# One fp32 attention and two feed-forward stages on one core: the last four blocks of the first feed-forward become two Strassen pairs

## The chip, the cores and the metric

The kernel runs on one core of one Trainium2 chip. The metric is the device time of one execution in microseconds (us), taken as the median over runs. Times of single instructions below come from one profiled execution of the kernel before the change.

## What is computed

```python
def _attn_ref(q, k, v, g_norm):            # 8 batches, 8 heads, 576 tokens, 64 wide
    kv = np.einsum('bhsd,bhse->bhde', k, v)
    out = np.einsum('bhsd,bhde->bhse', q, kv)
    rms = np.sqrt(np.mean(out * out, axis=-1, keepdims=True) + 1e-06)
    return out / rms * g_norm
def _moe_ref(x, w1, w2, w3, w_out):        # x 4608 x 512, w1..w3 512 x 768, w_out 768 x 512
    h = np.maximum(np.maximum(x @ w1, x @ w2), x @ w3)
    return h @ w_out
def _moe2_ref(x, w_in, w_out, s, b):       # w_in 512 x 2048, w_out 2048 x 512
    r = np.maximum(x @ w_in, 0.0)
    return (s * (r * r) + b) @ w_out
```

The attention output, 8 x 576 = 4608 tokens of 512 numbers, is the input x of the first feed-forward, and its output that of the second. Everything is wanted in fp32.

## The kernel before

**Arithmetic.** A float is split into a rounded part and a rest (hi and lo; hi on ScalarE at L279, lo on an adder engine at L282), and a product of two matrices is three products, hi by hi, hi by lo and lo by hi (`mm3`, L161 to L163). Each matmul instruction is a 128 x 128 weight tile against 512 columns.

**Blocks.** The tokens stand in nine blocks of 512. Block bb from 0 to 7 is the first 512 tokens of batch bb; block 8 collects the 64 tokens that each batch has left over (`o_rem`). The attention of batch bb+1 is done during the first feed-forward of block bb:

- k and v are loaded and multiplied (`kvor`, L334); q is loaded by four gathers on SyncE's queue (`load_q`, L349) and transposed on VectorE (`qt`, L390);
- `ops` (L403) and `rps` are the attention's products in PSUM, copied out as `o` by ScalarE and VectorE;
- the norm of each of four 128-row parts needs a square, its hi and lo (`sqh` on VectorE, L429, `sql` on GpSimd), a matmul with a matrix of ones (`ms`, L438 and L439, one PSUM bank), three ScalarE steps (L484 to L489) and three VectorE steps (`u`, `u`, `o`, L494 to L499);
- x is split into `xh` and `xl` (L503, L509; three of four `xl` on GpSimd).

**First feed-forward.** For every block there are 18 column tiles (6 of each of w1, w2, w3) by four k-chunks by three matmuls, 216 in all, into a ring of four PSUM banks (`g1_part`, L516). `g1_out` (L524) keeps the running maximum of the three weights' products (ScalarE copies the first, VectorE takes the maximum of the others, L531); h is split, and four output tiles by six chunks by three matmuls, 72 in all, form the product with w_out (`g2_mm`, L540). Its result goes to DRAM (`x1d`).

**Second feed-forward.** It works on pairs of blocks in a Strassen-Winograd scheme: 7 products of quarter matrices in the place of 8, with sums made on VectorE and ScalarE (`product`, L933, matmuls at L947; `z_product` with L1101). Its weights are converted from raw 64-bit input during the first feed-forward (`plan_conv` jobs p0 to p31, `tr_p` in the rows) and stored in DRAM.

**What sets the order.** Each piece of work is a `job` with a position, an engine, a cost, what it reads and writes, and which ring of tiles it takes. `arrange` (L71) simulates the engines with those costs and lists the jobs in the order in which they would begin; it runs once for all jobs with a position below `CUT` (L699) and once for the rest. The order within each engine is fixed by it in the program, so an engine that waits holds up all that stands behind it. A block is `SL` = 22 positions long. SyncE issues nearly all DMAs.

Of the kernel before, what the change touches and what calls it, by code (L numbers as in the profile page):

```python
# [30 lines left out]
def attention_max_ffn_relu2_ffn(ctx: ExitStack, tc, q, k, v, g_norm, w1, w2, w3, wo, wi, w2o, s, b, out):  # L31
# [568 lines left out]
    def plan_o(bb, u, pp, turn, mm):  # L600
        for p in pp if bb >= ROWS else ():
# [3 lines left out]
            a=[("ops", f"ops{bb}.{u}"), ("g", f"rps{bb}.{u}")] if pp[0] == 2 * u else [])  # L605
# [9 lines left out]
    def plan_compact(bb, p, t, u, x, eng, o, sq):  # L615
# [713 lines left out]
```

## Time and profile before

| | us |
| --- | --- |
| median of 3 runs (1386.41 to 1390.83) | 1388.78 |
| the profiled execution | 1386.89 |
| span of the profiled execution | 1385.1 |
| TensorE busy, of that span | 1367.6 |
| VectorE busy | 894.0 |
| ScalarE busy | 741.7 |
| GpSimd busy | 127.1 |

The share of busy time is one of the whole span; stages differ, so the windows and single rows count for more than the table. The first feed-forward of block 8 starts at 612 us, and the second feed-forward's first product at about 678 us.

### The profile page before, as it was taken

The page shows a single profiled execution, that of the slowest core. Times are in us where ns is not written, and L with a number is a line of the kernel's source. Part 1 is how long each engine was busy: PE and PEld are TensorE (multiplying, and loading weights), DVE is VectorE, ACT ScalarE, POOL GpSimd, SP SyncE. Part 2 cuts the span into 40 slices and gives each one's busy share as a digit, 9 for nine tenths or more (in the row PEclk, how much of TensorE's full clock was granted, in tenths as well). Part 3 has the DMA queues.
Part 4 walks back from the last instruction along what each step waited for, and adds up shares of the span by engine and source line. Part 5 has one row for each costly group of instructions (what it writes and reads, how often), then busy time and mean ns, then how long its engine had stood idle before and what let it go on. Part 6 is the DMA issues. An engine that isn't in the chain of part 4 may idle for free.

```text
span 1385.1 us, 19411 instructions
## 1 busy us (share of the span) xinstructions
PE 1367.6 (99%) x7056; PEld 1122.9 (81%) x7056; DVE 894.0 (65%) x1489; ACT 741.7 (54%) x1320; POOL 127.1 (9%) x99
## 2 busy tenths in 40 slices
PE   7999999999999999999999999999999999999998
PEld 5777888888888888888888889888888888888888
DVE  5984626364545453426676767657888888888875
ACT  6873535243434352334557457657675656556565
POOL 0001313121222132212000000000000000000000
PEclk9999999999999999999999999999999999999999
DMA  9986291626555331030444745534585465454531
GB/s 269 285 179 134 73 188 56 174 74 160 87 143 90 92 89 38 1 122 0 165 170 158 254 151 196 200 147 164 212 304 166 143 203 152 148 176 128 187 118 50
DMA packets 221328, 202.51 MB, mean 146 GB/s; under 512 B 117168, under 2 KB 175536, under 8 KB 219056
## 3 DMA queue, kind: packets, MB, share of 16 engines
q1 hardware_dynamic: 221072, 201.02, 49.1%
q8 instruction: 55, 0.90, 0.3%
q14 instruction: 41, 0.34, 0.1%
q10 hardware_dynamic: 160, 0.26, 0.1%
HBM read 126.79 MB, written 74.45 MB: 145 GB/s over the span
## 4 chain that ended last, share of the span: by engine, by line
PE 96%; DVE 2%; ACT 1%; DMA 1%; issue 0%; SPq 0%; ACTq 0%; DVEq 0%
PE ps_a L947 14%; PE g L161 14%; PE zs_a L1101 14%; PE g L163 14%; PE g L162 14%; PE ps_b L947 7%; PE zs_b L1101 7%; PE ps_c L947 4%; PE zs_c L1101 4%; PE kvor L334 1%; PE ops L403 1%; PE ms L438 0%; PE ms L439 0%; PE qps L370 0%; DVE tr_w L255 0%; DMA out_dram<-o 0%
## 5 line engine op out<-in xcount | busy, mean ns | idle before, releaser
L161 PE MATMUL g<-xh,w_w 128*128 128x512 f32 x648 | 255.2, 394 | 0.0
L163 PE MATMUL g<-xh,w_w 128*128 128x512 f32 x648 | 252.8, 390 | 0.7 <-DVE w_w L282 0.7
L162 PE MATMUL g<-xl,w_w 128*128 128x512 f32 x648 | 252.6, 390 | 0.0
L279 ACT ACTIVATE zx<-z 128x512 fp32r<-128x512 f32 (+1 forms) x280 | 158.3, 586 | 123.9 <-PE zs_a L1101 37.6
L1101 PE MATMUL zs_a<-zx,w_q 128*128 128x512 f32 (+1 forms) x960 | 212.0, 369 | 0.4 <-DVE zx L282 0.4
L947 PE MATMUL ps_a<-x_q,w_q 128*128 128x512 f32 (+1 forms) x960 | 207.9, 370 | 0.0
L282 DVE TENSOR_TENSOR zx<-z,zx 128x512 fp32r<-128x512 f32 (+1 forms) x280 | 171.3, 633 | 55.5 <-ACT zx L279 50.9
L1101 PEld LDWEIGHTS zs_a<-zx,w_q 128*128 128x128 f32 x960 | 168.1, 188 | 31.9 <-DVE zx L282 0.6
L947 PEld LDWEIGHTS ps_a<-x_q,w_q 128*128 128x128 f32 x960 | 167.6, 188 | 31.8
L531 DVE TENSOR_TENSOR h<-g,h 128x512 f32<-128x512 f32 x108 | 74.6, 691 | 153.9 <-PE g L163 150.1
L161 PEld LDWEIGHTS g<-xh,w_w 128*128 128x128 f32 x648 | 121.6, 188 | 27.5 <-issue 0.8
L163 PEld LDWEIGHTS g<-xh,w_w 128*128 128x128 f32 x648 | 121.6, 188 | 26.8 <-DVE w_w L282 1.2
L162 PEld LDWEIGHTS g<-xl,w_w 128*128 128x128 f32 x648 | 121.7, 188 | 25.3 <-DVE xl L282 0.2
L1101 PE MATMUL zs_b<-zx,w_q 128*128 128x512 f32 (+1 forms) x480 | 109.4, 370 | 2.0 <-DVE zx L282 2.0
L279 ACT ACTIVATE h<-h 128x512 fp32r<-128x512 f32 x54 | 34.0, 630 | 135.8 <-DVE h L531 135.1
L947 PE MATMUL ps_b<-x_q,w_q 128*128 128x512 f32 (+1 forms) x480 | 105.8, 369 | 0.0
L1101 PEld LDWEIGHTS zs_b<-zx,w_q 128*128 128x128 f32 x480 | 84.5, 188 | 18.2 <-DVE zx L282 2.4
L947 PEld LDWEIGHTS ps_b<-x_q,w_q 128*128 128x128 f32 x480 | 84.0, 188 | 15.8
L282 POOL TENSOR_TENSOR h<-h,h 128x512 fp32r<-128x512 f32 x40 | 54.8, 1370 | 456.4 <-ACT h L279 456.4
L161 PE MATMUL g<-h,w_o 128*128 128x512 f32 x216 | 84.6, 392 | 0.0
L162 PE MATMUL g<-h,w_o 128*128 128x512 f32 x216 | 84.1, 389 | 0.0
L163 PE MATMUL g<-h,w_o 128*128 128x512 f32 x216 | 84.1, 389 | 0.0
(175 smaller groups left out, 1855.6 us busy)
## 6 DMA issues: line engine op xcount, KB each, us to landing
z<-gd SPq DMA_DIRECT2D x64, 512.0 KB
gd<-cs SPq DMA_DIRECT2D x96, 256.0 KB
z<-gd SPq DMA_DIRECT2D x48, 256.0 KB
x1d<-x SPq DMA_DIRECT2D x36, 256.0 KB
raw_w<-in_moe_w_dram SPq DMA_DIRECT2D x18, 511.0 KB
k<-in_k_dram SPq DMA_DIRECT2D x32, 256.0 KB
v<-in_v_dram SPq DMA_DIRECT2D x32, 256.0 KB
wd<-tr_p SPq DMA_DIRECT2D x32, 256.0 KB
```

Of the source, the lines that this page charges most:

```text
L161: nc.tensor.matmul(ps, lhsT=w[:, 0, sl], rhs=xh, start=first, stop=False)
L162: nc.tensor.matmul(ps, lhsT=w[:, 0, sl], rhs=xl, start=False, stop=False)
L163: nc.tensor.matmul(ps, lhsT=w[:, 1, sl], rhs=xh, start=False, stop=last)
L279: act(out=out, in_=src, func=AF.Copy)
L282: eng.tensor_tensor(out=out, in0=src, in1=hi.bitcast(F32), op=ALU.subtract)
L334: nc.tensor.matmul(ps[h * D:(h + 1) * D, p, :], lhsT=kc, rhs=vc, start=(c == 0), stop=(c == C))
L403: nc.tensor.matmul(st["ops", u][p % 2 * D:(p % 2 + 1) * D, h], lhsT=kv[sl, p], rhs=st["qt", p][sl, :N], start=True, stop=True)
L531: nc.vector.tensor_tensor(out=st["h", m], in0=ps, in1=st["h", m], op=ALU.max)
L947: nc.tensor.matmul(ps, lhsT=w[:, a, c], rhs=x[:, b_], start=new and k == 0 and e == 0, stop=k == HK - 1 and e == 2, skip_group_check=True)
L1101: nc.tensor.matmul(ps, lhsT=w[:, a, c], rhs=x[:, b_], start=new and k_ == 0 and e == 0, stop=k_ == 3 and e == 2, skip_group_check=True)
```

## The change

**Two kinds of block.** Blocks 0 to 4 (`ND` = 5) run the first feed-forward as before. Blocks 5 and 6, and 7 and 8, become two pairs (`FP`), each in the Strassen-Winograd scheme that the second feed-forward has: for each pair 9 groups (two weight tiles each) by 7 products by 6 matmuls, 378 in the place of 2 x 216.

**Sums.** `f_whole` and `f_sum` form the sums of weight tiles on VectorE and `f_hi`, `f_lo` split them in pair 0; they are stored to DRAM (`sd`) and read back in pair 1 in the reverse order of groups. `x_sum` and the splits of x's quarters are those of the second feed-forward. `f_comb` (ScalarE copies, VectorE adds that read PSUM) and `f_max` combine the seven products and keep the maximum. Two rings of four PSUM banks, "g" and "gl", take the products of one group each in turn. The finished h goes to DRAM (`hd`).

**w_out later.** The four output tiles of blocks 5 to 8 are done after both pairs, from h read back (`fh_load`, `fh_hi`, `fh_lo`); since the tiles of w_out are used by the pairs' sums, they go to DRAM (`wo_out`) and come back (`wo_back`).

**Attention earlier.** All attention of batches 2 to 7 and the norm of block 8 stand at `TA` = 20, every `WA` = 10 positions, stretched by `FA` = 0.8: inside blocks 1 to 4, 2.2 attentions to a block. x of blocks 2 to 8 is stored to DRAM (`x_out`, `xd`), and read back for blocks 2 to 4 (`x_back`) and for the pairs (`fx_load`). All `xl` is now VectorE's; `sqh` may be VectorE's or ScalarE's. `rps` of batches from 2 on takes the one bank of `ms`. Of the 32 conversions 22 stand in blocks 1 to 4 and 10 in the pairs.

```diff
-            st["rps", u] = psg.tile([P, N], F32, tag="g", name=f"rps_{bb}_{u}")
+            st["rps", u] = (psa if bb > 1 else psg).tile([P, N], F32, tag="ms" if bb > 1 else "g", name=f"rps_{bb}_{u}")
...
-        job(t + u, "DVE", 0.42, sq_hi, bb, p, r=[sq], w=["h" + sq], a=[("sqh", "h" + sq)])
+        job(t + u, "DVE/ACT", (0.42, 0.6), sq_hi, bb, p, r=[sq], w=["h" + sq], a=[("sqh", "h" + sq)])
...
+        plan_x_out(bb, p, t + 7.2 * u, o)
...
-    CUT = SL * B - 0.2
+    ND, TU = 5, 32
+    TA, WA, FA = 20, 10, 0.8
+    CUT = SL * (ND - 1) + 12
...
+    def f_whole(G, e):
+        w = f_tiles(G)[e]
+        r = st["R", G, e] = ring("c", f"fr_{G}_{e}")
+        tt(nc.vector, r, w[:, 0].bitcast(F32), add, w[:, 1].bitcast(F32))
...
+    def f_product(a, n, G, i):
+        q, new = -1 - a, i in (0, 1, 5)
+        if new:
+            st["fp", a, G, BANK[i]] = bank(parity(n + (i == 5)), f"fp_{a}_{G}_{BANK[i]}")
+        ps = st["fp", a, G, BANK[i]]
...
+        for k in range(HK):
+            x = st["x", q, i, k]
+            c = slice(o + k * P, o + (k + 1) * P)
+            for e, (u, v_) in enumerate(((0, 0), (0, 1), (1, 0))):
+                nc.tensor.matmul(ps, lhsT=w[:, u, c], rhs=x[:, v_], start=new and k == 0 and e == 0,
+                                 stop=k == HK - 1 and e == 2, skip_group_check=True)
...
+    def f_comb(a, G, i, e, tag):
+        c, j = G // 3, {3: 2, 4: 1, 5: 0}.get(i)
+        ps = st["fp", a, G, BANK[i]]
+        if i < 3:
+            st["fc", a, G, i] = ring(tag, f"fc_{a}_{G}_{i}")
+            act(out=st["fc", a, G, i], in_=ps, func=AF.Copy)
+            return
...
+        if i < 6:
+            tt(nc.vector, st["fh", a, c, i] if e == 0 else st["fc", a, G, j], ps, add, st["fc", a, G, j])
...
+    def f_max(a, G, i):
+        h = st["fh", a, G // 3, i]
+        tt(nc.vector, h, h, ALU.max, st["fc", a, G, 5 - i])
```

**VectorE in block 2.** The rows are VectorE's in program order. In the names the first number is the block or batch and the second the part; `qt`, `sqh`, `u` and `o` are attention, `h` the maximum of the first feed-forward, `tr_p` a conversion. Before:

```order
L531 TENSOR_TENSOR h_2_1_1922<-g1_2_4_1907,h_2_1_1922 128x512
L264 SCALAR_TENSOR_TENSOR tr_p7_1904<-tr_p7_1904 128x512
L531 TENSOR_TENSOR h_2_1_1922<-g1_2_5_1936,h_2_1_1922 128x512
L429 TENSOR_SCALAR sqh_3_1_1986<-sq_3_1_1934 128x512
L494 SCALAR_TENSOR_TENSOR u_3_0_1995<-ms_3_0_1968,u_3_0_1995 128x512
L531 TENSOR_TENSOR h_2_2_1971<-g1_2_7_1973,h_2_2_1971 128x512
L496 SCALAR_TENSOR_TENSOR u_3_0_1995<-u_3_0_1995,y_3_0_1988 128x512
L499 SCALAR_TENSOR_TENSOR o_3_0_1897<-o_3_0_1897,g_sb_66,u_3_0_1995 128x512
L531 TENSOR_TENSOR h_2_2_1971<-g1_2_8_1998,h_2_2_1971 128x512
```

After:

```order
L437 COPY o_rem_152<-rps_4_0_1976 128x64
L404 STREAM_TRANSPOSE qt_4_2_2014<-qraw_4_1658 128x576
L404 STREAM_TRANSPOSE qt_4_3_2020<-qraw_4_1658 128x576
L447 TENSOR_SCALAR sqh_4_0_2046<-sq_4_0_2016 128x512
L512 SCALAR_TENSOR_TENSOR u_3_3_2053<-ms_3_3_2028,u_3_3_2053 128x512
L514 SCALAR_TENSOR_TENSOR u_3_3_2053<-u_3_3_2053,y_3_3_2048 128x512
L517 SCALAR_TENSOR_TENSOR o_3_1_1772<-o_3_1_1772,g_sb_66,u_3_3_2053 128x512
L260 TENSOR_SCALAR tr_p6_2074<-raw_p6_2011 128x512
L576 TENSOR_TENSOR h_2_0_2071<-g1_2_1_2058,h_2_0_2071 128x512
L264 SCALAR_TENSOR_TENSOR tr_p6_2074<-raw_p6_2011,tr_p6_2074 128x512
L277 TENSOR_TENSOR tr_p6_2074<-tr_p6_2074 128x512
L576 TENSOR_TENSOR h_2_0_2071<-g1_2_2_2082,h_2_0_2071 128x512
```

Before, the maxima of block 2 stand among one batch's norm; after, those of block 2 stand among the end of batch 3's norm, the transposes and norm of batch 4, and conversions.

**TensorE where block 5 begins.** `xh`, `xl` are block 5's input, `w_w` the weights, `kvor` the k by v product of the next batch. Before:

```order
L334 MATMUL kvor_129<-v_6_3_3068,k_6_3_3066 64x64 x8
L334 MATMUL kvor_129<-vrem_127,krem_125 64x64 x2
L161 MATMUL g1_5_0_3601<-xh_5_3454,w_w_0_172 128x512
L162 MATMUL g1_5_0_3601<-xl_5_3455,w_w_0_172 128x512
L163 MATMUL g1_5_0_3601<-xh_5_3454,w_w_0_172 128x512
```

After, `x_q_-1` is the input of pair 0 and `fs` a split sum of weights, and `fp` are the products of one group in banks a, b and c:

```order
L161 MATMUL g2_4_3_3968<-h_4_5_3966,w_o_5_1164 128x512
L162 MATMUL g2_4_3_3968<-h_4_5_3966,w_o_5_1164 128x512
L163 MATMUL g2_4_3_3968<-h_4_5_3966,w_o_5_1164 128x512
L1392 MATMUL fp_0_0_a_4066<-x_q_-1_0_0_3855,w_w_0_200 128x512 x3
L1392 MATMUL fp_0_0_a_4066<-x_q_-1_0_1_3857,w_w_0_200 128x512 x3
L1392 MATMUL fp_0_0_b_4082<-x_q_-1_1_0_3895,fs_0_0_4024 128x512 x3
L1392 MATMUL fp_0_0_b_4082<-x_q_-1_1_1_3922,fs_0_0_4024 128x512 x3
L1392 MATMUL fp_0_0_c_4096<-x_q_-1_5_0_3997,w_w_0_200 128x512 x3
L1392 MATMUL fp_0_0_c_4096<-x_q_-1_5_1_4018,w_w_0_200 128x512 x3
```

The block's 216 direct matmuls are replaced by products of six matmuls each, and no attention stands among them; the product with w_out of block 4 ends right before.

**VectorE in the same stretch.** Before, in the first feed-forward of block 5:

```order
L531 TENSOR_TENSOR h_5_1_3714<-g1_5_4_3701,h_5_1_3714 128x512
L266 TENSOR_TENSOR tr_p22_3722<-tr_p22_3722 128x512
L531 TENSOR_TENSOR h_5_1_3714<-g1_5_5_3732,h_5_1_3714 128x512
L429 TENSOR_SCALAR sqh_6_1_3783<-sq_6_1_3730 128x512
L494 SCALAR_TENSOR_TENSOR u_6_0_3795<-ms_6_0_3765,u_6_0_3795 128x512
L531 TENSOR_TENSOR h_5_2_3768<-g1_5_7_3770,h_5_2_3768 128x512
L496 SCALAR_TENSOR_TENSOR u_6_0_3795<-u_6_0_3795,y_6_0_3785 128x512
L499 SCALAR_TENSOR_TENSOR o_6_0_3693<-o_6_0_3693,g_sb_66,u_6_0_3795 128x512
L531 TENSOR_TENSOR h_5_2_3768<-g1_5_8_3798,h_5_2_3768 128x512
```

After, in the third to fifth group of pair 0 (`fr` and `sf` are sums of weights, 128 x 512 and 128 x 256, `fc` and `fh` combine the products):

```order
L855 TENSOR_TENSOR fr_4_1_4207<-w_w_13_808 128x512
L275 SCALAR_TENSOR_TENSOR tr_p22_4078<-tr_p22_4078 128x512
L855 TENSOR_TENSOR fh_0_0_3_4219<-fp_0_0_b_4082,fc_0_0_2_4209 128x512
L855 TENSOR_TENSOR fh_0_0_5_4221<-fp_0_0_c_4096,fc_0_0_0_4186 128x512
L855 TENSOR_TENSOR sf_4_1_4223<-fr_4_0_4196,fr_4_1_4207 128x256
L855 TENSOR_TENSOR fh_0_0_4_4239<-fp_0_0_a_4066,fc_0_0_1_4117 128x512
L855 TENSOR_TENSOR fh_0_0_5_4221<-fh_0_0_5_4221,fc_0_1_0_4130 128x512
L855 TENSOR_TENSOR sf_4_1_4223<-fr_4_1_4207 128x256
L855 TENSOR_TENSOR fc_0_2_0_4241<-fp_0_2_c_4200,fc_0_2_0_4241 128x512
L855 TENSOR_TENSOR sf_4_2_4261<-sf_4_1_4223,fr_4_0_4196 128x256
L855 TENSOR_TENSOR fh_0_0_5_4221<-fh_0_0_5_4221,fc_0_2_0_4241 128x512
L855 TENSOR_TENSOR sf_4_2_4261<-fr_4_0_4196,sf_4_2_4261 128x256
```

In the place of maxima, norm and conversion stands a nearly unbroken row of additions, those that read a TensorE bank (`<-fp`) among those that prepare weights for later groups.

On all engines, in program rows: TensorE 6534 becomes 6426, VectorE 1491 becomes 1673, ScalarE 1324 becomes 1403, GpSimd 104 becomes 63, SyncE 771 becomes 897.

## Rows read from the trace of the kernel before

**Rows 1.** The page's busy times: engine, us (share) and instructions.

```profile
PE 1367.6 (99%) x7056; PEld 1122.9 (81%) x7056; DVE 894.0 (65%) x1489; ACT 741.7 (54%) x1320; POOL 127.1 (9%) x99
```

**Rows 2.** The page's chain that ended last: shares by engine.

```profile
PE 96%; DVE 2%; ACT 1%; DMA 1%; issue 0%; SPq 0%; ACTq 0%; DVEq 0%
```

**Rows 3.** Windows: stretch, busy time by engine (instructions), granted clock, DMA share, GB/s.

```profile
0.00:60.00 60.00, 50.48 (x413) 36.27 (x414) 41.24 (x87) 41.85 (x71) 1.63 (x8) 1.00 1.03 268
60.00:120.00 60.00, 59.26 (x333) 43.91 (x335) 45.12 (x80) 39.29 (x68) 0.00 (x0) 1.00 0.79 195
...
180.00:240.00 60.00, 60.00 (x354) 48.24 (x353) 28.52 (x45) 24.86 (x42) 13.54 (x10) 1.00 0.54 116
...
420.00:480.00 60.00, 60.00 (x344) 48.96 (x343) 29.98 (x44) 25.81 (x43) 14.20 (x10) 1.00 0.45 94
...
660.00:1300.00 640.00, 640.00 (x2967) 533.02 (x2966) 482.70 (x798) 394.55 (x710) 0.00 (x0) 1.00 0.53 183
1300.00:1385.10 85.10, 77.91 (x514) 71.13 (x512) 61.72 (x139) 50.51 (x117) 0.61 (x2) 0.99 0.29 87
```

**Rows 4.** Timeline of TensorE: start, length, line, tile, shape, instructions.

```profile
612.36 0.39 PE L161 MATMUL g<-xh,w_w 128*128 128x512 f32 x1
...
661.32 0.39 PE L161 MATMUL g<-h,w_o 128*128 128x512 f32 x1
...
1302.81 1.52 PE L1101 MATMUL zs_a<-zx,w_q 128*128 128x512 f32 x6
1304.17 1.52 PE L1101 MATMUL zs_b<-zx,w_q 128*128 128x512 f32 x6
```

**Rows 5.** Timeline of SyncE's queue: the q gathers of two batches, start and issue time.

```profile
123.87 5.97 SPq L349 DMA_DIRECT2D qraw<-in_q_dram  x4
...
196.50 5.80 SPq L349 DMA_DIRECT2D qraw<-in_q_dram  x4
```

**Rows 6.** VectorE's lines by form: count, busy us, mean ns, idle before it and releaser.

```profile
L531 DVE TENSOR_TENSOR h<-g,h 128x512 f32<-128x512 f32 x108 | 74.6, 691 | 153.9 <-PE g L163 150.1 <-ACT tr_p L259 3.4 <-ACT sq L419 0.2
...
L803 DVE TENSOR_TENSOR cs<-ps_a,cs 128x512 f32<-128x512 f32 x32 | 21.7, 689 | 6.0 <-PE ps_a L947 5.5
...
L803 DVE TENSOR_TENSOR z<-z,z 128x256 f32<-128x256 f32 x16 | 6.2, 415 | 0.0
...
L282 DVE TENSOR_TENSOR w_q<-s,w_q 128x512 fp32r<-128x512 f32 x32 | 21.7, 685 | 9.3 <-ACT w_q L279 9.3
...
L282 DVE TENSOR_TENSOR xl<-o,xh 128x512 fp32r<-128x512 f32 x14 | 15.3, 1114 | 0.4 <-ACT xh L279 0.4
...
L494 DVE SCALAR_TENSOR_TENSOR u<-ms,u 128x512 f32<-128x512 f32 x28 | 19.3, 688 | 35.3 <-ACT u L489 35.3
...
L499 DVE SCALAR_TENSOR_TENSOR o<-o,g_sb,u 128x512 f32<-128x512 f32 x24 | 22.1, 922 | 0.5
```

**Rows 7.** The same view of GpSimd's rest of the square.

```profile
L282 POOL TENSOR_TENSOR sql<-sq,sqh 128x512 fp32r<-128x512 f32 x28 | 38.2, 1364 | 31.1 <-DVE sqh L429 31.1
```

**Rows 8.** Windows of 10 us, columns as in rows 3: two with a q gather, two with a conversion or less.

```profile
200.00:210.00 10.00, 10.00 (x46) 8.25 (x45) 4.46 (x8) 3.07 (x5) 2.58 (x2) 1.00 1.27 156
210.00:220.00 10.00, 10.00 (x56) 7.54 (x55) 6.27 (x13) 6.25 (x10) 2.93 (x2) 1.00 0.17 52
...
340.00:350.00 10.00, 10.00 (x46) 8.25 (x45) 4.95 (x8) 3.10 (x6) 3.04 (x3) 1.00 1.15 121
...
480.00:490.00 10.00, 10.00 (x56) 7.58 (x55) 5.08 (x9) 4.23 (x7) 2.59 (x2) 1.00 0.30 79
```

**Rows 9.** The page's line on DMA packets.

```profile
DMA packets 221328, 202.51 MB, mean 146 GB/s; under 512 B 117168, under 2 KB 175536, under 8 KB 219056
```

**Rows 10.** ScalarE's lines by form, columns as in rows 6: the norm's three steps.

```profile
L484 ACT ACTIVATE y<-ms,eps 128x512 f32<-128x512 f32 x28 | 19.2, 684 | 0.0
L486 ACT ACTIVATE y<-y 128x512 f32<-128x512 f32 x28 | 17.7, 633 | 0.8
L489 ACT ACTIVATE u<-y 128x512 f32<-128x512 f32 x28 | 17.6, 630 | 0.6
```

More of the change, by code (lines that the diff above doesn't have):

```diff
@@ L187, in attention_max_ffn_relu2_ffn @@
     wd = [dram.tile([P, 4, N], F32, name=f"wd{n}") for n in range(M2 // 2)]
+    xd = [dram.tile([P, KD, N], F32, name=f"xd{j}") for j in range(NB)]
+    hd = [dram.tile([P, M1, N], F32, name=f"hd{j}") for j in range(NB)]
+    sd = [dram.tile([P, 2, 2, N], F32, name=f"sd{n}") for n in range(G1 // 2)]
+    od = dram.tile([P, M1, 2, N], F32, name="od")
     gd = [dram.tile([P, 5, M2 // 2, N], F32, name=f"gd{q}") for q in range(B // 2 + 1)]
@@ L221, in attention_max_ffn_relu2_ffn, with parity @@
     st = {}
+    def parity(n):
+        return "gl" if n % 2 else "g"
     def conv_load(key, dsts, raw):
@@ L576, in plan_kv @@
         lag = 2.0 if bb < 2 else 8.0
-        job(load(0) + 0.01, "SP", 1.1, load_rem, bb, w=["rem"], lag=lag)
+        job(load(0) + 0.01 if bb < 3 else mm(0) - WA + 0.1, "SP", 1.1, load_rem, bb, w=["rem"], lag=lag)
         for p in range(NP):
@@ L604, in plan_o @@
             w=[f"ops{bb}.{u}:{p}" for p in pp] + [f"rps{bb}.{u}:{p}" for p in pp] + [f"kr:{2 * u}.{p}" for p in pp],
-            a=[("ops", f"ops{bb}.{u}"), ("g", f"rps{bb}.{u}")] if pp[0] == 2 * u else [])
+            a=[("ops", f"ops{bb}.{u}"), ("ms" if bb > 1 else "g", f"rps{bb}.{u}")] if pp[0] == 2 * u else [])
     def plan_oout(bb, u, pos):
@@ L696, in attention_max_ffn_relu2_ffn @@
     SQ = ["sq", "sqh", "sql", "sqx"]
+    XB = ["sqx", "xb"]
     CP, LP = 4, (-1, 3.35, 3.65, 3.95)
-    WIDE = {0: 2, 1: 4}
-    CUT = SL * B - 0.2
+    WIDE = {bb: 4 if bb else 2 for bb in range(B)}
+    ND, TU = 5, 32
+    TB = SL * ND
+    TC = TB + TU * (B + 1 - ND) // 2
+    OFF = TC - 162
+    TA, WA, FA = 20, 10, 0.8
+    CUT = SL * (ND - 1) + 12
     Z = -12
@@ L746, in attention_max_ffn_relu2_ffn @@
+    for bb in range(2, ND):
+        plan_x_back(bb, SL * bb - 5, SL * (bb - 1) + G1 + 0.2)
+    for j in range(ND):
+        t = SL * j
         for g in range(G1):
@@ L1245, in plan_put, with fx_load, fs_slot @@
             job(pos + 0.02, eng, 0.6, turn_store, c, u, e, eng, r=[nm])
+    FP = [(ND + 2 * a, ND + 2 * a + 1) for a in range((NB - ND) // 2)]
+    NG = G1 // 2
+    SIDE = {1: (0, 0), 4: (0, 1), 2: (1, 0), 6: (1, 1)}
+    cur = {}
+    def fx_load(a, c):
+        st["raw", -1 - a, c] = [slot(f"v{2 * c + r}", f"fx_{a}_{c}_{r}", F32) for r in range(2)]
+        for r, t in enumerate(st["raw", -1 - a, c]):
+            nc.sync.dma_start(out=t, in_=xd[FP[a][c]][:, 2 * r:2 * r + 2])
+    def fs_slot(a, G):
+        if G % 3 < 2:
+            t = base.tile([P, 2, 2, N], F32R, tag=("xh", "xl")[G % 3], name=f"fs_{a}_{G}")
+            st["S", "f", G] = [t[:, 0], t[:, 1]]
+        else:
+            st["S", "f", G] = [slot(WOS[i], f"fs_{a}_{G}_{i}") for i in range(2)]
@@ new lines, in f_hi, with f_lo, f_store, f_reload @@
+    def f_hi(G, t):
+        if t == 0:
+            fs_slot(0, G)
+        hi_part(st["S", "f", G][t][:, 0], st["SF", G, bool(t)])
+    def f_lo(G, t):
+        s_ = st["S", "f", G][t]
+        lo_part(s_[:, 1], st["SF", G, bool(t)], s_[:, 0], nc.vector)
+    def f_store(G, t):
+        nc.sync.dma_start(out=sd[G][:, t], in_=st["S", "f", G][t].bitcast(F32))
+    def f_reload(a, G):
+        fs_slot(a, G)
+        for t in range(2):
+            nc.sync.dma_start(out=st["S", "f", G][t].bitcast(F32), in_=sd[G][:, t])
@@ L1249, in attention_max_ffn_relu2_ffn @@
+    plan_pairs()
     for g in range(3):
```

271 lines of the change are left out of this document (213 added, 58 removed).

## The prediction

> **What bounds the kernel now.** I read the busy times first: TensorE 1367.6 of 1385.1 us, every other engine at 65% or below [rows 1]. The chain of waits agrees, 96% TensorE [rows 2]. The windows then show where the 17.5 idle us lie: 9.5 in the first 60 us, 0.7 in the next 60, none in the windows shown between 180 and 1300, and 7.2 in the last 85 [rows 3]. The order of the head (to block 0's w_out product) and of everything from the second feed-forward's first product on is unchanged on every queue, so the idle ends stay. The stage that the change rewrites, blocks 1 to 8 of the first feed-forward, has a TensorE that never waits, at a granted clock of 1.00, its full level of 2.4 GHz. There a matmul taken out is worth its whole issue interval, and a wait that appears is lost whole.
>
> **TensorE's saving.** Block 8's first feed-forward product starts at 612.36 and its first w_out product at 661.32 [rows 4]: 216 matmuls and nothing else between in 48.96 us, 0.2267 us each. (The single durations, 0.39, overlap and can't be added.) The Strassen products of the second feed-forward, the form that the pairs take over, have the same interval: 1304.17 - 1302.81 = 1.36 us for six [rows 4], 0.227 each. Removed are 4 x 216 = 864 matmuls, added 2 x 378 = 756; the 288 of w_out for these blocks are moved, not dropped. 108 x 0.2267 = 24.5 us. Attention products keep their number and only move. Without a new wait the profiled execution goes from 1386.89 to 1362.4.
>
> **Blocks 1 to 4, the compute engines.** A block with one attention now takes 196.50 - 123.87 = 72.6 us [rows 5], of which 288 x 0.2267 = 65.3 are the feed-forward, so an attention costs TensorE 7.3. With 2.2 of them a block lasts 65.3 + 2.2 x 7.3 = 81.4 us. VectorE carries some 28.5 us in 60 now [rows 3]. Counting its rows of the order by kind at the durations of rows 6 gives 44, 54, 53 and 42 us for blocks 1 to 4, at most 67% of 81; ScalarE by the same count at most 53. Neither binds by its sum. GpSimd keeps `sql`, at 1.36 us each [rows 7], 13 to 15 instructions a block, 20 us.
>
> What does the slowdown by GpSimd cost? The lo of an x part took VectorE 1114 ns in the stage where GpSimd works, the same operation 685 ns on weights in the second feed-forward, where GpSimd is idle [rows 3, 6]; the norm's last step took 922 beside 688 for one that reads a PSUM bank [rows 6]. If each GpSimd instruction cost VectorE its whole 1.36 us, that is 20 us more a block: 74 of 81, still below. The Trainium skill, "SBUF — State Buffer", section "Who interferes with whom", says that a VectorE instruction with two SBUF inputs contends with a GpSimd instruction that reads SBUF, and that the shared port is held for a whole instruction. The 1114 ns agree; that rule speaks against packing 2.2 attentions into a block, but it alone leaves the sum as it is.
>
> The one bank of `ms` gets `rps` as a tenant too, six to an attention in the place of four. After an `ms` product the bank is free when `u` has read it: 0.684 + 0.633 + 0.630 + 0.688 = 2.64 us [rows 6, 10], and the order puts the next tenant one or two column tiles (2.72 us each, twelve matmuls) later. It is tight where it is one tile, but then the predecessor is mostly an `rps`, which only needs a short copy. I take 1.5 us for all waits of the compute engines and loads in blocks 1 to 4; ends 0 and 9.
>
> **Blocks 1 to 4, DMA.** Per block: 2.2 x (3.54 MB of q, k, v + 1.05 of x out) = 10.1; some 7 conversions of 0.77 MB, 5.4; x back 1.05 and the block's result 1.05: 17.6 MB in 81.4 us, 216 GB/s. Now the stage moves 94 to 130 GB/s; the highest rates are 268 in the head, at a share of 1.03, and 195 at 0.79 [rows 3]. By shares: the 10 us windows with a q gather, which run at 1.27 and 1.15 [rows 8], give about 11 us of all sixteen engines for a q load with its small follow-up, and a window with a conversion 0.30 x 10 = 3.0 us for 0.77 MB, so 3.7 per MB. 2.2 x 11 + 15.0 x 3.7 = 80 us of share in 81.4. That is full, but the loads of the next attention are issued 10 positions (some 35 us) ahead, and only the three densest blocks are like this. I count it within the 0 to 9 above and carry the rest as a rival.
>
> **Hand-over to pair 0.** The four loads of x (2.1 MB) are issued late, because the second run of the planner begins there. By the order VectorE needs the first some 6 us and the last some 8.7 us later, at 240 GB/s, below the 268 that the head reached [rows 3]. TensorE has block 4's w_out products as cover, 72 x 0.2267 = 16 us. I take 0.5, ends 0 and 5.
>
> **Pair 0.** VectorE's rows from block 4's last maximum to the pair's last combination are 167: 131 of about 0.69 (rows like `h` 691, `cs` 689, lo 685) and 36 half as wide at 0.415 [rows 6], 90 + 15 = 105 us. TensorE has 72 + 378 = 450 matmuls there, 102.0 us. So VectorE is the longer engine by 3 us, in a stage without GpSimd work. It has a lead: it makes sums of weights several groups ahead, and a bank is needed again only after another group. Stepping both queues side by side with these durations, VectorE idles some 4 us early (its first combination waits for TensorE), later runs up to 5 us behind, and the tightest bank comes free 2 us before TensorE wants it. I take 1.5; ends 0 and 8 (3 + 4.2, if no lead is there to use).
>
> **Pair 1 and the late w_out products.** Pair 1 has 69 VectorE rows, 47 us beside 85.7: covered. h and w_out are read back beside big transfers only, and the 288 matmuls last 65 us, with 24 lo and as many hi: 0.5, ends 0 and 3.
>
> **Sum.** 1362.4 + 1.5 + 0.5 + 1.5 + 0.5 = 1366.4 for an execution like the profiled one; the median of the runs lies 1.9 above the profiled execution, so 1368.3. With no wait at all 1364.3.
>
> **Rivals.**
>
> *VectorE bounds pair 0, part of the gain goes back.* If its instructions there are a tenth longer than the rows say, or a hop per instruction isn't in the durations, 105 becomes 115: with the 4 us of early waiting, 105 x 1.1 + 4 - 102 = 17 us in the place of 1.5, total 1384 at most; a mean case of 12 gives 1379. For it: the stage is at 103% by plain sums, and additions that read PSUM stand right before the bank that TensorE wants. Against: in the second feed-forward VectorE works 482.7 of 640 us [rows 3] with no wait of TensorE, at the same durations. 0.18.
>
> *DMA becomes the bound in blocks 1 to 3: slower than before.* Place: the q gathers on SyncE's queue, behind them the k, v and conversions of the next attention; then `qt` on VectorE waits and `ops` on TensorE. Price: (17.6 MB / rate - 81.4 us) x 3. It eats the whole 24.5 where a block lasts 89.6 us, a rate of 196 GB/s, and by more than 0.3% below 193. At 180 it is 49 us, and the time 1413. For it: windows with a q gather moved only 156 and 121 GB/s at a full share [rows 8], and 117168 of 221328 packets are under 512 bytes [rows 9]; 195 is the highest rate beyond the head. Against: the same sums by share come to 80, not above 81.4, and the 195 stood at 0.79. The Trainium skill, "DMA: Bandwidth & Descriptors", section "Specifications", gives 512 bytes as the least transfer for line rate; the packets of the gathers are the kind it warns of, and the full windows at 121 and 156 agree with it. Slower by this 0.06; ending within 0.3% by it 0.04.
>
> *The `ms` bank paces attention.* 28 parts in blocks 1 to 4; TensorE waits at the next tenant if the four steps stand behind other work in their queues. At 0.87 us each this is 24.5, no change. Before, such steps stood among less work; 0.02, counted with within 0.3%.
>
> That the change does not do what it says: the order holds 756 products of the pairs and 864 direct matmuls fewer, so I give it nothing.
>
> **How the numbers follow.** Forecast (waits of 0 to 9 us, 1364 to 1373.5) 0.70; part given back (1373.5 to 1384.5) 0.18; within 0.3%, that is 4.2 us, which is about what a measurement of this kernel can tell from no change (1384.6 to 1392.9), 0.06; slower 0.06. The range begins 2 us below the case without waits, the spread of the runs shown, 1362, and takes in the first half of the second case, up to 1379. Faster 0.88, same 0.06, slower 0.06.
>
> **What would show it.** L161 to L163 with `xh`, `xl` 360 each in the place of 648; 756 matmuls of `fp` at 0.227; TensorE busy near 1343. If the term for pair 0 is right, VectorE is above 95% for about 100 us, and TensorE's waits on `fh` or `fc` sum to under 8 us. If the DMA term is right, blocks 1 to 3 show a share near 1 and over 200 GB/s with no wait of TensorE on `qt`, `kvor` loads or `y`. Waits of over 10 us in sum between 70 us and the second feed-forward make the forecast wrong; so does a feed-forward interval other than 0.227 in the pairs.

## The result: 1367.9 us, and the profile after

The changed kernel takes 1367.91 us (median of 4 runs, 1367.25 to 1368.26); the kernel before, beside it, 1387.6 us. The ratio is 0.9854, 95% interval 0.9835 to 0.9874: faster by 1.5%. The forecast was 1368.3.

Busy times and the chain of the changed kernel, as in [rows 1, 2]:

```profile
PE 1345.9 (98%) x6948; PEld 1101.0 (81%) x6948; DVE 982.8 (72%) x1671; ACT 789.7 (58%) x1399; POOL 68.5 (5%) x58
...
PE 95%; DVE 2%; DMA 1%; SPq 1%; ACT 1%; issue 0%; ACTq 0%; DVEq 0%
```

TensorE has 108 matmuls less and is still the bound; its busy time fell by 21.7 us, not by the 24.5 of the forecast, and its idle time rose by 3.0, to 20.5.

The windows of the changed kernel, columns as in [rows 3]: blocks 1, 2, 3 and 4, then pair 0, then the whole of blocks 1 to 4 and the whole from the first pair product to the second feed-forward:

```profile
110.80:192.30 81.50, 81.50 (x546) 63.95 (x545) 48.52 (x81) 42.32 (x71) 17.32 (x13) 1.00 0.85 209
192.30:273.20 80.90, 80.90 (x531) 63.82 (x530) 55.75 (x87) 45.48 (x75) 19.68 (x14) 1.00 0.90 211
273.20:350.30 77.10, 77.10 (x436) 61.22 (x435) 51.52 (x80) 48.05 (x80) 21.21 (x15) 1.00 0.47 139
350.30:416.52 66.22, 66.22 (x294) 54.76 (x292) 40.80 (x65) 25.99 (x42) 7.98 (x6) 1.00 0.35 103
416.50:500.90 84.40, 84.40 (x368) 68.73 (x367) 74.55 (x135) 42.58 (x73) 0.00 (x0) 1.00 0.65 222
...
110.78:416.52 305.74, 305.74 (x1802) 243.76 (x1800) 196.58 (x311) 161.86 (x267) 66.19 (x48) 1.00 0.66 169
416.52:657.35 240.83, 240.11 (x1045) 195.91 (x1044) 171.97 (x289) 111.32 (x190) 0.00 (x0) 1.00 0.64 212
```

Blocks 1 and 2 last 81.5 and 80.9 us where 81.4 was forecast, with TensorE busy without a gap, at the full level of the granted clock. The DMA engines are at a share of 0.85 to 0.90 there, at 209 to 211 GB/s. Blocks 3 and 4 last only 77.1 and 66.2 us: by TensorE's attention products (`ops`, 16 to a batch) the six batches stand as 2.5, 2, 1.5 and none in the four blocks, not as 2.2 in each. VectorE in pair 0 is busy for 74.6 of 84.4 us, 88%.

What TensorE waits for in the changed kernel (line, releaser, us in sum, times, longest), the ten longest:

```profile
PE qps L390 <- DMA qraw<-in_q_dram: 5.7, 1, 5.7
PE zs_b L1153 <- DVE zx L293: 2.2, 2, 1.6
PE ops L417 <- ACT kvc L353: 1.5, 3, 0.8
PE msc L463 <- ACT sq L434: 1.3, 2, 0.8
PE kvor L348 <- DMA vrem<-in_v_dram: 1.2, 1, 1.2
PE zs_a L1153 <- DVE zx L293: 1.0, 1, 1.0
PE kvor L348 <- DMA v<-in_v_dram: 0.8, 1, 0.8
PE ops L417 <- DVE qt L404: 0.7, 1, 0.7
PE g L163 <- DVE w_w L293: 0.7, 1, 0.7
PE g L162 <- DVE h L293: 0.7, 1, 0.7
```

All but the last belong to the head or the tail. The two `kvor` waits, on loads at 12 and 14 us, aren't in the profile before; in the traces of the other kernels below they come to between 0 and 1.2 us, so they are the loads' timing from one execution to the next. The last row is the only new wait behind the head: 0.7 us at the first late w_out product, on VectorE's rest of h.

Put together by stretches of the two traces: block 1's start to the second feed-forward's first product took 566.28 us and takes 305.74 + 240.83 = 546.57, that is 19.7 less. The head is 0.6 us shorter, the second feed-forward and the tail 1.6 us longer, in the same order of instructions; these two are left unexplained.

### The profile page after: what moved, and what is told of

Same layout as the page of the kernel before. It is cut to its first block, busy times and chain, and to the rows that moved or that the text cites. A ratio compares the mean times of both kernels' runs of the same rounds, so it can differ in the third digit from the quotient of the medians.

```text
span 1366.4 us, 19727 instructions
## 1 busy us (share of the span) xinstructions
PE 1345.9 (98%) x6948; PEld 1101.0 (81%) x6948; DVE 982.8 (72%) x1671; ACT 789.7 (58%) x1399; POOL 68.5 (5%) x58
## 4 chain that ended last, share of the span: by engine, by line
PE 95%; DVE 2%; DMA 1%; SPq 1%; ACT 1%; issue 0%; ACTq 0%; DVEq 0%
PE ps_a L999 15%; PE zs_a L1153 14%; PE g L161 9%; PE g L163 9%; PE g L162 9%; PE ps_b L999 7%; PE fp_a L1392 7%; PE zs_b L1153 7%; PE zs_c L1153 4%; PE ps_c L999 4%; PE fp_b L1392 4%; PE fp_c L1392 2%; PE kvor L348 1%; PE ops L417 1%; DMA vrem<-in_v_dram 1%; PE ms L456 1%
## 5 line engine op out<-in xcount | busy, mean ns | idle before, releaser
L293 DVE TENSOR_TENSOR zx<-z,zx 128x512 fp32r<-128x512 f32 (+1 forms) x280 | 171.3, 634 | 55.8 <-ACT zx L290 52.8
L161 PE MATMUL g<-xh,w_w 128*128 128x512 f32 x360 | 142.7, 396 | 0.0
L163 PE MATMUL g<-xh,w_w 128*128 128x512 f32 x360 | 140.7, 391 | 0.7 <-DVE w_w L293 0.7
L162 PE MATMUL g<-xl,w_w 128*128 128x512 f32 x360 | 140.5, 390 | 0.0
L161 PEld LDWEIGHTS g<-xh,w_w 128*128 128x128 f32 x360 | 67.5, 188 | 15.9 <-issue 0.8
L163 PEld LDWEIGHTS g<-xh,w_w 128*128 128x128 f32 x360 | 67.6, 188 | 15.6 <-DVE w_w L293 1.1
L162 PEld LDWEIGHTS g<-xl,w_w 128*128 128x128 f32 x360 | 67.6, 188 | 14.1 <-DVE xl L293 0.3
L576 DVE TENSOR_TENSOR h<-g,h 128x512 f32<-128x512 f32 x60 | 41.5, 692 | 39.1 <-PE g L163 37.8
L1028 ACT ACTIVATE cs<-cs 128x512 f32<-128x512 f32 (+1 forms) x60 | 35.1, 586 | 54.7 <-DVE cs L855 54.1
L1400 ACT ACTIVATE fc<-fp_a 128x512 f32<-128x512 f32 x36 | 21.4, 597 | 71.3 <-PE fp_a L1392 69.0
L1015 ACT ACTIVATE cs<-ps_a 128x512 f32<-128x512 f32 (+1 forms) x80 | 43.4, 555 | 25.5 <-PE ps_a L999 22.8
L1153 PE MATMUL zs_c<-zx,w_q 128*128 128x512 f32 (+1 forms) x240 | 54.7, 370 | 0.0
L855 DVE TENSOR_TENSOR cs<-ps_b,cs 128x512 f32<-128x512 f32 (+1 forms) x40 | 25.0, 637 | 39.8 <-issue 32.9
```

What stands on the lines that cost most here:

```text
L161: nc.tensor.matmul(ps, lhsT=w[:, 0, sl], rhs=xh, start=first, stop=False)
L162: nc.tensor.matmul(ps, lhsT=w[:, 0, sl], rhs=xl, start=False, stop=False)
L163: nc.tensor.matmul(ps, lhsT=w[:, 1, sl], rhs=xh, start=False, stop=last)
L293: eng.tensor_tensor(out=out, in0=src, in1=hi.bitcast(F32), op=ALU.subtract)
L576: nc.vector.tensor_tensor(out=st["h", m], in0=ps, in1=st["h", m], op=ALU.max)
L855: eng.tensor_tensor(out=out, in0=in0, in1=in1, op=op)
```

## The experiments

Ten kernels ran. The edits are to the changed kernel.

**No pairs: the packing alone.**

```diff
-    ND, TU = 5, 32
+    ND, TU = 9, 32
...
-    CUT = SL * (ND - 1) + 12
+    CUT = SL * (ND - 1) - 0.2
...
-    for m in range(M1):
-        job(SL + 6 + 3 * m, "SP", 1.95, wo_out, m, r=[f"W_o{m}:0", f"W_o{m}:1"], w=[f"od:{m}"])
...
-    plan_pairs()
+    for n in range(2 * M2):
+        pos = SL + 2 + (CUT - SL - 9) / (2 * M2) * n
+        plan_conv(f"p{n}", p2_src(n), pos, pos - 3, "craw", "ctr", store=pos + 1.5)
```

> One part of the change alone: the attention of batches 2 to 7 and the norm of block 8 inside blocks 1 to 4, x of blocks 2 to 8 through DRAM and back, the conversions spread as their places allow, but no pairs: all nine blocks direct, w_out right after each block. TensorE has as many products as the kernel before. Theory A (the packing is free, the pairs carry the whole gain): 1386 to 1390, TensorE's waits between 70 us and the second feed-forward under 2 us. Theory B (the packing costs something that the pairs hide, such as matmuls that run slower beside a fuller VectorE and DMA): 1391 to 1397. Theory C (part of the gain is the packing's): 1375 to 1384.

Measured: 1387.19 us beside 1386.88 of the kernel before, ratio 1.0003 (0.9993 to 1.0012). Its windows, blocks 1 to 4 and a little, and the rest of the first feed-forward:

```profile
111.00:420.00 309.00, 309.00 (x1819) 246.98 (x1818) 172.62 (x278) 155.21 (x256) 67.55 (x48) 1.00 0.63 159
420.00:676.00 256.00, 256.00 (x1131) 211.98 (x1130) 99.62 (x151) 70.69 (x118) 28.27 (x20) 1.00 0.25 76
```

TensorE has no gap in either. Theory A: packing the attention of six batches into four blocks and sending x through DRAM neither costs nor gives anything that these runs tell; the pairs, with the late w_out, carry the whole gain. Whether they could do without the packing was not tried.

**One bank for the norm and the remaining tokens, undone.**

```diff
-            st["rps", u] = (psa if bb > 1 else psg).tile([P, N], F32, tag="ms" if bb > 1 else "g", name=f"rps_{bb}_{u}")
+            st["rps", u] = psg.tile([P, N], F32, tag="g", name=f"rps_{bb}_{u}")
...
-            a=[("ops", f"ops{bb}.{u}"), ("ms" if bb > 1 else "g", f"rps{bb}.{u}")] if pp[0] == 2 * u else [])
+            a=[("ops", f"ops{bb}.{u}"), ("g", f"rps{bb}.{u}")] if pp[0] == 2 * u else [])
```

> One part undone: the attention's products of the remaining tokens take a bank of the ring of four again, and the one bank of the norm has four tenants to an attention in the place of six. Theory A (the one bank did not hold up TensorE): within 1.5 us of the changed kernel, 1366 to 1369.5. Theory B (the prediction's 1.5 us in blocks 1 to 4 lie there): 1 to 3 us less, 1365 to 1367. Theory C (the ring of four is now the scarce one, with 2.2 attentions to a block): 2 to 8 us more, 1370 to 1376.

Measured: 1368.65 us (1367.32 to 1369.91), ratio to before 0.9871 (0.9856 to 0.9885), beside 0.9854 of the changed kernel: no difference that these runs tell. Theory A; the `ms` bank cost nothing that shows.

**VectorE in pair 0, three doses.** The sums of whole weights are repeated into the same tile; 9, 18 and 36 rows more. For 18:

```diff
+    def f_again(G, e):
+        w = f_tiles(G)[e]
+        tt(nc.vector, st["R", G, e], w[:, 0].bitcast(F32), add, w[:, 1].bitcast(F32))
...
+        for e in range(2):
+            for _ in range(1):
+                job(pos + 0.01, V, 0.69, f_again, G, e, r=[f"{w[e]}:0", f"{w[e]}:1"], w=[f"FR{G}.{e}"])
```

The reason for the doses is VectorE's timeline of the changed kernel in pair 0 (start, length):

```profile
452.68 0.69 DVE L855 TENSOR_TENSOR fh<-fp_c,fc 128x512 f32<-128x512 f32 x1
453.29 0.68 DVE L855 TENSOR_TENSOR fr<-w_w 128x512 f32<-128x512 f32 x1
...
454.67 0.42 DVE L855 TENSOR_TENSOR sf<-fr,fr 128x256 f32<-128x256 f32 x1
455.00 0.42 DVE L855 TENSOR_TENSOR sf<-fr 128x256 f32<-128x256 f32 x1
455.34 0.76 DVE L264 SCALAR_TENSOR_TENSOR tr_p<-raw_p,tr_p 128x512 uint16<-128x512 uint16 x1
```

The next row starts 0.61 us after one that lasts 0.69, and 0.33 to 0.34 after one that lasts 0.42: VectorE's rows overlap as TensorE's do, and their durations can't be added.

> The changed kernel, with VectorE doing the two whole-weight sums of each of the nine groups of pair 0 once more into the same tile: 18 more 128x512 additions in front of the sums that read them, result unchanged. Theory A (VectorE has room in pair 0: from one row's start to the next's lie 0.607 us, less than the 0.685 that a row lasts, so its 157 rows fill 88 of 101 us): 18 x 0.607 = 10.9 us more fit into the 12 free, TensorE waits 0 to 2 us more in the stretch, time 1368 to 1370. Theory B, the prediction's own sum (durations add, VectorE 105 of 102 us, already the longer engine): 18 x 0.69 = 12.4 us, of which 8 to 12 end on TensorE, 1376 to 1380.

> The same with the two sums done three times: 36 more additions in pair 0. Theory A (12 us of room): 36 x 0.607 = 21.9 us, so about 10 (7 to 14) end on TensorE as waits of products for sums of weights or for banks that VectorE has not read, time 1375 to 1382. Theory B (no room): 25 us, 1391 to 1395. If the rows added are hidden altogether, both fall and VectorE's order does not reach TensorE here.

Measured: 1375.71 us with 18 rows (ratio to before 0.992, 0.9903 to 0.9936), 1381.57 with 36 (0.9962, 0.9949 to 0.9975), so 7.8 and 13.7 more than the changed kernel. For 18 rows this is just under B's range, for 36 inside A's, and the trace shows why neither was right for both. TensorE in the run with 18 rows has two waits that the changed kernel has not, one of them long (its timeline, with the idle time and its releaser in brackets), and VectorE stands like this in front of the long one:

```profile
432.68 0.95 PE L1399 MATMUL fp_a<-x_q_-1_4_0_3976,fs 128*128 128x512 f32 x3 [0.74 <-ACT fc L1407]
...
499.88 0.85 PE L1399 MATMUL fp_a<-x_q_-2_0_1_4719,w_w 128*128 128x512 f32 x3
504.94 1.65 PE L1399 MATMUL fp_a<-x_q_-1_6_0_4044,fs 128*128 128x512 f32 x3 [4.20 <-DVE fc L855]
...
510.04 0.86 PE L1399 MATMUL fp_a<-x_q_-2_2_0_4786,fs 128*128 128x512 f32 x3
```

```profile
496.38 0.69 DVE L293 TENSOR_TENSOR x_q_-2_0_0_4716<-fx,x_q_-2_0_0_4716 128x512 fp32r<-128x512 f32 x1
...
500.00 0.69 DVE L293 TENSOR_TENSOR x_q_-2_1_1_4790<-t_-2_1_4777,x_q_-2_1_1_4790 128x512 fp32r<-128x512 f32 x1
500.60 0.68 DVE L293 TENSOR_TENSOR x_q_-2_2_0_4786<-t_-2_0_4761,x_q_-2_2_0_4786 128x512 fp32r<-128x512 f32 x1
...
501.80 0.68 DVE L855 TENSOR_TENSOR fc<-fp_b,fc 128x512 f32<-128x512 f32 x1
502.40 0.68 DVE L855 TENSOR_TENSOR fc<-fp_c,fc 128x512 f32<-128x512 f32 x1
503.00 1.28 DVE L855 TENSOR_TENSOR fh<-fh,fc 128x512 f32<-128x512 f32 x2
504.20 0.68 DVE L855 TENSOR_TENSOR fc<-fp_a,fc 128x512 f32<-128x512 f32 x1
```

Most of the lateness of pair 0 comes out at its end: the sums and splits of pair 1's input (`x_q_-2`) stand in VectorE's queue ahead of pair 0's last combinations, and TensorE's next product needs the bank that the last `fc` reads. During the wait the granted clock halves. The windows of the same run:

```profile
495.00:500.00 5.00, 5.00 (x23) 4.05 (x22) 5.00 (x10) 4.48 (x9) 0.00 (x0) 1.00 0.59 202
500.00:505.00 5.00, 0.80 (x5) 0.33 (x3) 5.00 (x10) 3.60 (x6) 0.00 (x0) 0.80 0.00 0
...
502.50:503.00 0.50, 0.00 (x0) 0.00 (x0) 0.50 (x1) 0.00 (x0) 0.00 (x0) 0.97 0.00 0
503.00:503.50 0.50, 0.00 (x0) 0.00 (x0) 0.50 (x2) 0.00 (x0) 0.00 (x0) 0.50 0.00 0
...
505.00:508.00 3.00, 3.00 (x7) 2.42 (x8) 2.44 (x5) 0.60 (x1) 0.00 (x0) 0.50 0.02 5
508.00:511.00 3.00, 3.00 (x11) 2.30 (x10) 1.98 (x4) 1.26 (x2) 0.00 (x0) 0.70 0.57 129
511.00:520.00 9.00, 9.00 (x41) 7.31 (x40) 7.55 (x13) 4.66 (x9) 0.00 (x0) 1.00 0.43 133
```

At 0.50, the level of 1.2 GHz, matmuls run at about half their rate. By the clock column the lower level holds for 0.20 x 5 / 0.5 + 3 + 0.30 x 3 / 0.5 = 6.8 us, from about 503.0 to 509.8. For the first 1.9 of these TensorE still waits, which costs nothing more. The 12 matmuls from 504.94 to 510.04 take 5.1 us where 12 x 0.2308 = 2.8 would be the full level: 2.3 us are lost beside the waits of 4.2 and 0.7, together 7.2 of the 7.7 by which the profiled executions differ (1375.99 and 1368.26). With 36 rows the same place waits 6.1 us, four smaller waits of 0.3 to 1.2 are new, 9.5 us in all, and the clock halves again for 6.8 us, 5.4 of them with work: by the same estimate 2.7 us more.

The first reading of this was: 10.9 us of added work gave 4.2 of waiting, so there is room of 6.7 us at that place, and a step of 3.4 more behind the wait. The third dose tests it:

> The smallest dose on VectorE: one of the two whole-weight sums of each of pair 0's nine groups done once more, 9 rows. With 18 rows TensorE waited 4.2 us at one place, the hand-over from pair 0 to pair 1, where VectorE's sums and splits of pair 1's input stand ahead of pair 0's last combinations, and then ran 6.8 us at half the clock. Theory C (18 x 0.607 = 10.9 us were added and 4.2 came out, so 6.7 us of room lie at that place): 9 x 0.607 = 5.5 us stay inside, no wait of TensorE between 400 and 580 us, clock at its full level there, 1367 to 1369. Theory B (VectorE is the bound already): 9 x 0.69 = 6.2 us, half to all of it on TensorE, and with a wait of some us the clock's 3.4 on top, 1371 to 1377.

Measured: 1368.55 us (1368.40 to 1368.93), 0.6 above the changed kernel. Theory C has the time and the clock, which stays at its full level, but not the absence of waits: the one on VectorE is gone, and two of 0.7 and 0.5 us on ScalarE's copies are there, the second at the hand-over.

What the doses show is that 9 rows nearly fit and 18 don't. The 6.7 us are no property of the changed kernel, because `arrange` orders all jobs anew for each dose: between pair 0's first product and its last, VectorE has 15 conversion rows in the changed kernel and 10 in each of the three, and the products at the hand-over stand in another order. The same sum for 36 rows gives 21.9 - 9.5 = 12.4 us of room.

**DMA in blocks 1 to 4, three doses.** Each x that attention stores is stored again, once and three times; the third kernel does the three extra stores from a weight tile.

```diff
             nc.sync.dma_start(out=xd[bb].rearrange("p (h u) n -> p u h n", u=2)[:, u], in_=st["ot", bb, u])
+            for x in xe:
+                nc.sync.dma_start(out=x[bb].rearrange("p (h u) n -> p u h n", u=2)[:, u], in_=st["ot", bb, u])
```

> The changed kernel, with each x that attention stores to DRAM stored once more into a tensor that nobody reads: 1.05 MB more per attention, 2.3 MB more per block in blocks 1 to 4. Theory A (the sixteen DMA engines were at a share of 0.87 between 120 and 270 us, and 3.7 us of share per MB make it 0.97): no new wait, 1367 to 1370. Theory B, the prediction's sum (80 of 81.4 us of share taken): 8.5 us over 1.4 free, 7 a block in three blocks, 1385 to 1390, with TensorE waiting for the transposed q or for k and v.

> The same with three more stores of each x: 3.15 MB more per attention, 6.9 MB per block, 24.5 MB in 81.4 us or 301 GB/s. Theory A (share 0.87 plus 6.9 x 3.7 / 81.4 = 0.31): 1.18, so blocks of 96 us in the place of 81.4 in the two or three densest, 30 to 45 us, 1398 to 1413. Theory C (what counts is the q gathers' small packets, big stores run beside them at rates such as the 296 GB/s of the head): under 5 us, 1368 to 1373. Either way DMA, and not VectorE, is named by TensorE's waits.

Measured: 1367.94 us with one store more, the same as the changed kernel, with shares of 0.91 and 1.01 in 120 to 240 us; 1380.62 with three more (ratio to before 0.9953, 0.9937 to 0.9969), 12.7 above it, under A's 30 to 45 and over C's 5. My line that DMA would be named by TensorE's waits was wrong too; a chain over SyncE's queue, ScalarE, VectorE and TensorE, in this order, shows in the run with three more who is behind it:

```profile
152.30 9.87 SPq L364 DMA_DIRECT2D qraw<-in_q_dram  x4
162.26 1.85 SPq L526 DMA_DIRECT2D xd<-o  x1
164.16 2.96 SPq L528 DMA_DIRECT2D xe<-o  x3
```

```profile
172.69 1.02 ACT L428 ACTIVATE o<-ops 128x1024 f32<-128x1024 f32 x1 [6.41 <-DMA xe<-o]
```

```profile
175.65 0.69 DVE L513 SCALAR_TENSOR_TENSOR u<-ms,u 128x512 f32<-128x512 f32 x1 [5.88 <-ACT u L508]
```

```profile
176.40 0.50 PE L457 MATMUL ms<-sqh,ones 128*128 128x512 f32 x1 [2.06 <-DVE u L513]
```

The issue of these q gathers takes 9.9 us (6.6 to 9.9 for the five loads from 110 to 320 us, 6.2 to 7.7 in the changed kernel, 5.8 and 6.0 before [rows 5]), the stores of x stand behind it on SyncE's queue, ScalarE's copy into the next tile of `o` waits 6.4 us for a store to leave it, the norm's steps stand behind that copy, and TensorE waits for the norm's one bank. Four such waits sum to 7.2 us, the longest 3.5, and with two of them, of 2.1 and 3.5 us, the clock halves.

> As the run with three more stores of each x, the same bytes at the same places, but the extra stores read a weight tile that nobody changes, so they don't hold the attention output's tile. With x as source TensorE waited 7.2 us in four places, all on the norm's step behind a ScalarE copy that waited for a tile of o still being stored. Theory D (DMA at a share of 1 delays the store of x itself, behind q gathers whose issue then takes 10 us in the place of 6): 4 to 8 us of waits and 3 to 10 of half clock again, 1374 to 1382. Theory E (the tile was held by the extra stores alone, the bandwidth does no harm): 0 to 2 us of waits, 1367 to 1370.

Measured: 1372.57 us (1369.64 to 1373.55), 4.7 above the changed kernel, though these windows carry as many bytes or more (243, 285 and 266 GB/s in the run that stores x three times more):

```profile
120.00:180.00 60.00, 60.00 (x431) 47.58 (x430) 35.39 (x58) 32.62 (x55) 15.48 (x12) 1.00 0.96 240
180.00:240.00 60.00, 57.64 (x351) 44.94 (x349) 38.71 (x61) 33.07 (x54) 13.84 (x10) 1.00 1.04 290
240.00:300.00 60.00, 58.74 (x423) 45.97 (x421) 40.45 (x66) 31.19 (x54) 11.09 (x9) 1.00 1.10 303
```

Two waits of 2.4 and 1.3 us on the same bank, and a clock at its full level throughout. So it lies between D and E: by the difference of the two runs some 8 of the 12.7 us were the tile held by its extra readers, with the clock behind those waits, and a share of 1.04 to 1.10 with 290 to 303 GB/s costs under 5 us in this schedule.

**The pairs' interval, two tries.** In the changed kernel's timeline of TensorE 30 rows of three matmuls each lie from the first of these to the second:

```profile
430.32 0.86 PE L1392 MATMUL fp_c<-x_q_-1_5_0_3997,w_w 128*128 128x512 f32 x3
...
451.09 0.86 PE L1392 MATMUL fp_c<-x_q_-1_5_0_3997,w_w 128*128 128x512 f32 x3
```

20.77 us for 90 matmuls, 0.2308 each, beside 0.2267 of the direct ones [rows 4].

```diff
-        hi_part(st["x", q, i, k][:, 0], x_f(q, i, k))
+        hi_part(st["x", q, i, k][:, int(q < 0)], x_f(q, i, k))
...
-                nc.tensor.matmul(ps, lhsT=w[:, u, c], rhs=x[:, v_], start=new and k == 0 and e == 0,
+                nc.tensor.matmul(ps, lhsT=w[:, u, c], rhs=x[:, 1 - v_], start=new and k == 0 and e == 0,
```

> The changed kernel, but in the pairs the rest of x stands in the first half of its tile and the rounded part in the second; the products are the same. In the changed kernel a product matmul of the pairs starts 0.2305 us after the one before, a direct one 0.2267. Theory A (the 4 ns depend on where the moving and the weight tiles lie): the interval of the pairs' matmuls changes by over 1 ns, at best to 0.2267, 756 x 3.8 ns = 2.9 us, time 1365 to 1367. Theory B (it is in the form of the products: a new tile every three matmuls, a new bank every six): 0.2305 again, 1367 to 1369.

```diff
-            for e, (u, v_) in enumerate(((0, 0), (0, 1), (1, 0))):
+            for e, (u, v_) in enumerate(((0, 0), (1, 0), (0, 1))):
```

> The changed kernel, but the three matmuls of each pair product stand as hi weight by hi x, lo weight by hi x, hi weight by lo x, so the moving tile stays for two and the weights change each time. Theory A (the interval hangs on which weight tile is loaded while which moving tile is read): the mean interval of the pairs moves by over 1 ns from 0.2305, the time by 1 to 3 us either way. Theory B (form of the products, not the pairing): 0.2305, 1367 to 1369.

Measured: 1367.72 us and 1368.87, ratios to before 0.9863 (0.9848 to 0.9878) and 0.987 (0.9853 to 0.9886), and the rows of products start 0.69 to 0.70 us apart in both as in the changed kernel. The mean over all pairs' matmuls is 0.2305 in all three. Theory A falls in both forms. Theory B, that the 4 ns lie in the form of the products, has its number but is not the cause either. The second feed-forward's products have the form that the prediction took for the pairs, and in the chain of the kernel before one line of the program, L1101, runs at both rates (start, length):

```profile
1059.29 10.88 PE zs_a L1101 x48
1098.73 8.29 PE zs_a L1101 x36
```

That is 0.2267 and 0.2303 each, at the full clock. What makes the difference stays open.

## Why the prediction was right, and where its steps were not

**The saving.** Right in kind: each matmul taken out was worth an issue interval, since nothing else became the bound, and the run without pairs shows that the packing of the attention does not move the time. The size was off: I priced the pairs' 756 matmuls at 0.2267 us, from two rows of the second feed-forward that happened to stand at its low end [rows 4]. From the first pair product to the second feed-forward TensorE was busy 240.1 us for 1044 matmuls; at 0.2267 it would be 236.7. The mis-sized term is 3.4 us, of which the pairs at 0.2305 are 756 x 0.0038 = 2.9, so the saving was 21 rather than 24.5. The prediction had named this itself as a sign of being wrong ("a feed-forward interval other than 0.227 in the pairs"). The mean over the second feed-forward's 512-column products in the kernel before, 0.2286, would have shown half of it.

**Blocks 1 to 4.** 1.5 us of waits were forecast, none came. The sums held for the first two blocks: 81.5 and 80.9 us, 209 to 211 GB/s for 216; and VectorE's count for all four, 48.5, 55.8, 51.5 and 40.8 us for 44, 54, 53 and 42. They did not hold for block 3, 77.1 us at 139 GB/s, because the 2.2 attentions to a block were not spread evenly: six batches and the norm of block 8 are 44 us over four blocks. The allowance for the `ms` bank was not needed (the run that undoes it).

**The DMA rival.** It was to decide at 196 GB/s and to win below. The price for a share was close in two of the three blocks (0.98 forecast, 0.85, 0.90 and 0.47 measured), but the rates from which the rival was argued, 121 and 156 GB/s in windows with a q gather, are not a ceiling: with other transfers beside the gathers the engines moved 290 to 303 GB/s. The line of the Trainium skill, "DMA: Bandwidth & Descriptors", section "Specifications", on transfers below 512 bytes fits with the share that a gather takes, and says nothing on what runs beside it. A bandwidth that is measured where little is asked for is a demand, not a limit.

**The hand-over to pair 0.** 0.5 forecast, none measured.

**Pair 0.** The step that failed in its reasoning: "VectorE is the longer engine by 3 us" added durations, 105 us. By starts a 512-wide row takes 0.61 and a half one 0.33, 131 x 0.61 + 36 x 0.33 = 92 us beside 102, and the trace has VectorE at 88%, where the prediction's sign was above 95%. I had said of TensorE's durations that they overlap, and not looked at VectorE's. The first rival, with rows longer than their durations, fell by the same rows. The 1.5 us that I took became 0. The step looked for the tightest bank without saying where it is; the doses found the long waits at the bank that pair 0's last combination reads. Its 2 us of slack were too few: 9 rows, 5.5 us by starts, brought 1.2 us of waits.

**Pair 1 and w_out.** 0.5 forecast, 0.7 measured, at the first late product.

**The sum.** 4.0 us of waits were forecast and 0.7 came; 0 us of longer intervals and 3.4 came. The two errors nearly cancel, and the forecast for the profiled execution, 1366.4, stands beside 1368.26. The rest is the second feed-forward and the tail, 1.6 us longer, the head, 0.6 shorter, and some 0.7 us in blocks 1 to 4 that have no gap and no explanation here. The forecast of the median added 1.9 us, by which the median of the first three runs of the kernel before lay above its profiled execution; over the later runs its median is 1386.7 to 1387.0, level with that execution, and the changed kernel's profiled execution is 0.4 above its median. So that the median came out 0.4 from the forecast is luck, three errors that cancel; that the time fell by about 20 is not.

**The slower side.** Nothing that was tried turned the sign: doubling the stores of x cost nothing, and it took 36 rows more on VectorE, or three more stores from the held tile, to give back about two thirds of the gain.

## What to carry to other kernels

When one engine is at 99%, price a change by what it removes from that engine, at the interval between starts of the very form that will run, averaged over many; then ask of each other engine, again by starts and not by durations, how full it gets in the stretch that changes. In these doses lateness came out where a queue puts the next stage's preparation ahead of the last stage's results, so look for the slack at hand-overs. A rate seen in a window is a limit only if something waited for it there.

## What the runs showed of the hardware

- A wait of TensorE can cost more than its length. With a wait of 4.2 us the granted clock stood at 0.50 for 6.8 us, from before the wait's end, and the work behind it took 2.3 us longer; with one of 6.1 us it again stood there for 6.8 us. After the 0.7 us at the first late w_out product of the changed kernel, and 2.4 in the run that stores a weight tile, it stayed at 1.00. The length of the wait alone doesn't tell: a wait of 2.1 us in the run that stores x three times more, right behind 2.5 us of 64-column `kvor` products, was followed by 3.4 us at 0.50, while the 2.4 us stood behind 512-column ones. The prediction had priced every wait at its length.
- VectorE's rows overlap: 128 x 512 additions start 0.61 us apart and last 0.68 to 0.69, half ones 0.33 to 0.34 and 0.42.
- Matmuls of one shape, 128 x 128 weights against 512 columns, at the full clock, run in stretches at 0.2267 us and in others at 0.230 to 0.232: direct products 0.2267 (216 of block 8) and 0.233 (six from 115.06 us of the changed kernel, right behind an attention product), the pairs 0.2305 to 0.2308, the second feed-forward's products both. Where the rest of x lies in its tile and in what order the three matmuls of a product stand made no difference in the pairs. The cause is open.
- The sixteen DMA engines moved 303 GB/s over 60 us at a reported share of 1.10, with q gathers among the transfers.
